# Pooled attention and token mixer on one Trainium2 core: v summed by GpSimd in fp32, with another order of the first batch and one tail unit for each of the first batches

## The chip, the cores and the metric

One core of one Trainium2 chip. The metric is the device time of one execution in microseconds (us), lower is better. Engines as in the profile: PE is TensorE (PEld its weight loads), DVE VectorE, ACT ScalarE, POOL GpSimd, SP SyncE; SPq and POOLq are DMA issues.

## What is computed

Eight batches of eight heads, 576 tokens, 64 wide. k and v are averaged over groups of eight tokens (72 pooled rows), every q row attends to the 72, and the result, laid out as x (batch, token, 512), goes through a token mix and a channel mix:

```
k_p = k.reshape(B, H, 72, 8, D).mean(axis=3);  v_p likewise
attn = softmax(q @ k_p^T / sqrt(D));  x = attn @ v_p
u = x + (relu(x^T @ w_tok1) @ w_tok2)^T
out = u + relu(u @ w_ch1) @ w_ch2
```

Inputs and output are fp32; the kernel loads everything with a cast to bf16.

## The kernel before

The 576 tokens of a batch are 512 main tokens, four (NJ) on each of 128 partitions, and a tail of 64. Two tails share 128 partitions as a group: batches 0 and 7, 1 and 2, 3 and 4, 5 and 6 (`groups`; `slot_of` gives the upper or lower half). In the group of 0 and 7 each batch has a tail unit of its own; otherwise one `TailUnit` does both batches of a group with the first.

For a batch, `pool_k` averages k with small matmuls against a 0/1/8 matrix (line 241, tails 245) and copies the result into a block form `kbd` (ACT line 250, DVE 251, from one PSUM tile). `pool_v` averages v with four matmuls of 512 columns (line 258) and one for the tail (259); ACT copies to `vpx` (260), whose last column of ones yields the softmax denominators. A `Unit` has two of the four main token sets: `do_qT`, `do_S` (scores, line 286; maximum 289 and difference 291 on DVE), `do_E` (exponential, 299), `do_PT` (transposed probabilities) and `do_AV` (`values`, line 325, then reciprocal 329 and multiply 330 on DVE). Batches 0 and 1 transpose on PE (lines 275 and 310, copies 277 and 311), later ones by DMA issued on SP (`qT_dma`, line 472; line 306).

`token_mix` has `do_AT` (lines 414 and 418, ReLU 408 and 410), `do_u` (442, tail 450, sum 447) and `do_uT` (on PE with copies at 464 for batch 0, by SP DMA at 458 otherwise). `channel_mix` has `do_GT` (line 673, ReLU 675), which needs all of `uT`, and the output matmuls (688, sum 692, stores at 707).

The instruction order on each engine is that of the program: `weave` mixes a main stream (channel mix of batch b, `c_stream`) with a side stream (values and mixes of b+1, `value_stream`; scores of b+2, `score_stream`) by weights; `delay` holds the side back at the start, `lead` ends it early. `first_stream` is the attention and token mix of batch 0 alone, and `second_stream` that of batch 1, beside the channel mix of batch 0. `keep_running` issues matmuls on zeros.

GpSimd issues all loads (line 120 main, 124 tail), in order. k, q and v have two buffers each. Batches 1 and 2 are loaded up front; a later one behind a copy (`gate`, line 658) that waits for work two batches earlier:

```python
add(0, load_gated, 3, lambda: x_main[1][:, 0, 0:1])           # in second_stream
add(0, load_gated, b + 2, lambda: c.pT[1][:, 0, 0:1])         # in value_stream
```

Of the kernel before, what the change touches and what calls it, by code (L numbers as in the profile page):

```python
# [48 lines left out]
def kernel(  # L49
# [34 lines left out]
    kv_pool = ctx.enter_context(tc.tile_pool(name="kv", bufs=2))  # L84
    tail_pool = ctx.enter_context(tc.tile_pool(name="tl", bufs=2))
# [24 lines left out]
    for t in tail_t[0]:  # L110
        nc.vector.memset(t[half[1]], 0.0)

    def load(b):
        g = group_of[b]
        if g and slot_of[b] == 0:
            tail_t[g] = [tail_pool.tile([P, H, D], BF16, name=n) for n in ("kt", "qt", "vt")]
        main_t[b] = [kv_pool.tile([P, H, NJ, D], BF16, name=n) for n in ("km", "qm", "vm")]
        for i in (0, 2, 1) if slot_of[b] else (0, 1, 2):
            src, mt, tt = (k, q, v)[i], main_t[b][i], tail_t[g][i]
            nc.gpsimd.dma_start(out=mt.rearrange("p h j d -> p h (j d)"),  # L120
                                in_=src[b, :, 0:MAIN, :].rearrange("h (p j) d -> p h (j d)", j=NJ))

            for bb in [b] if g == 0 else groups[g] if slot_of[b] == 0 else []:
                nc.gpsimd.dma_start(out=tt[half[slot_of[bb]]], in_=src[bb, :, MAIN:S, :].rearrange("h p d -> p h d"))

    main_t[0] = [kv_pool.tile([P, H, NJ, D], BF16, name=n) for n in ("km", "qm", "vm")]
# [44 lines left out]

    NB = 3
    kbd = [singles.tile([P, H, 2, SP], BF16, name=f"kbd{i}") for i in range(NB)]
    vpx = [singles.tile([SP, H, D + 1], BF16, name=f"vpx{i}") for i in range(NB)]
    for i in range(NB):
        eng = nc.vector if i == 0 else nc.any
        eng.memset(kbd[i], 0.0)
        eng.memset(vpx[i][:, :, D], 1.0)
# [4 lines left out]
    x_tail[0] = singles.tile([P, DM], BF16, name="xt0")  # L183
    nc.any.memset(x_tail[0][half[1]], 0.0)
# [47 lines left out]
    def pool_k(b):  # L232
        g, s = group_of[b], slot_of[b]
        km, kt = main_t[b][0], tail_t[g][0]
        kp_ps = ps.tile([P, HP, SP], FP32, name="pa")
        if b == 0:
            keep_running(kp_ps.rearrange("p r n -> p (r n)"), 18)
        for pr in range(HP):
            for j in range(NJ):
                for hl in range(2):  # L240
                    nc.tensor.matmul(out=kp_ps[hl * D:(hl + 1) * D, pr, 0:SPM], lhsT=km[:, 2 * pr + hl, j, :],  # L241
                                     rhs=pool_m[:, 0:SPM], start=(j == 0), stop=(j == NJ - 1))
        for pr in range(HP):
            for hl in range(2):
                nc.tensor.matmul(out=kp_ps[hl * D:(hl + 1) * D, pr, SPM:SP], lhsT=kt[:, 2 * pr + hl, :],
                                 rhs=pool_t[s][:, SPM:SP], start=True, stop=True)
        heads = kbd[b % NB].rearrange("p (r t) e n -> p r t e n", t=2)
        for hl in range(2):
            src = kp_ps[hl * D:(hl + 1) * D]
            nc.scalar.copy(out=heads[0:D, :, hl, 0, :], in_=src)  # L250
            nc.vector.tensor_copy(out=heads[D:P, :, hl, 1, :], in_=src)  # L251

    def pool_v(b):
        g, s = group_of[b], slot_of[b]
        vm, vt = main_t[b][2], tail_t[g][2]
        vp_ps = ps.tile([SP, H, D], FP32, name="pa")
        for j in range(NJ):
            nc.tensor.matmul(out=vp_ps, lhsT=pool_m, rhs=vm[:, :, j, :], start=(j == 0), stop=False)  # L258
        nc.tensor.matmul(out=vp_ps, lhsT=pool_t[s], rhs=vt, start=False, stop=True)
        nc.scalar.copy(out=vpx[b % NB][:, :, 0:D], in_=vp_ps)  # L260

    class Unit:
# [40 lines left out]
        def do_PT(self, e):  # L303
            self.pT[e] = pt_pool.tile([P, H, P], BF16, name="pT")
            if not self.by_pe:
                nc.sync.dma_start_transpose(out=self.pT[e], in_=self.probs[:, e].rearrange("p h n -> p (h n)"))
                return
            pT_ps = ps_tr.tile([SP, H, P], BF16, name="pt")
            for h in range(H):
                nc.tensor.transpose(out=pT_ps[:, h, :], in_=self.probs[:, e, h, 0:SP], identity=ident)  # L310
            (nc.scalar.copy if self.first else nc.vector.tensor_copy)(out=self.pT[e][0:SP], in_=pT_ps)  # L311

        def do_AV(self, e):
            values(self.pT[e], x_main[self.b][:, 2 * self.jj + e, :], slice(0, P), [(slice(0, P), self.b)],
                   2 if self.first else 0)

    def values(pT, xo, rows, pieces, extra, place=lambda h: h):
        w = rows.stop - rows.start
        for hf in range(2):
            ao = ps.tile([P, HP, D + 1], FP32, name="pa")  # L320
            keep_running(ao.rearrange("p h d -> p (h d)"), extra)
            for hh in range(HP):
                h = hf * HP + hh
                for r, b in pieces:
                    nc.tensor.matmul(out=ao[r, hh, :], lhsT=pT[0:SP, place(h), r], rhs=vpx[b % NB][:, h, :],  # L325
# [8 lines left out]
    class TailUnit:  # L334
# [19 lines left out]
        def do_S(self):  # L354
            w = self.rows
            sc = [ps.tile([P, HP, SP], FP32, name="pa") for _ in range(2)]
            for pr in range(HP):
                for hl in range(2):
                    for b in self.bs:
                        r = half[slot_of[b]]  # L360
                        nc.tensor.matmul(out=sc[hl][r, pr, :], lhsT=self.qT[hl * D:(hl + 1) * D, pr, r],
# [3 lines left out]
            for hl in range(2):  # L365
                mx = sm_pool.tile([P, 8], FP32, name="mx")
                nc.vector.tensor_reduce(out=mx[w, 0:HP], in_=sc[hl][w], axis=AX.X, op=ALU.max)
                sh = sh_pool.tile([P, 6, SP], FP32, name="sh")
                nc.vector.tensor_tensor(out=sh[w, 0:HP], in0=sc[hl][w],
                                        in1=mx[w, 0:HP, None].broadcast_to([w.stop - w.start, HP, SP]),  # L370
# [3 lines left out]
        def do_E(self):  # L374
            w = self.rows
            self.probs = prob_t[self.g % 2]
            for hl in range(2):
                nc.scalar.activation(out=self.probs[w, hl, :, 0:SP], in_=self.sh[hl][w, 0:HP], func=AF.Exp, scale=scale)

        def do_PT(self):  # L380
            w = self.rows
            self.pT = pt_pool.tile([P, H, P], BF16, name="pT")
            if not self.by_pe:
                nc.sync.dma_start_transpose(out=self.pT, in_=self.probs.rearrange("p e h n -> p (e h n)"))
                return
            pT_ps = ps_tr.tile([SP, H, P], BF16, name="pt")
            for h in range(H):
                nc.tensor.transpose(out=pT_ps[:, self.place(h), w], in_=self.probs[w, h % 2, h // 2, 0:SP],
                                    identity=ident[w, w])
            copy = nc.scalar.copy if self.first else nc.vector.tensor_copy  # L390
            copy(out=self.pT[0:SP, :, w], in_=pT_ps[:, :, w])

        @staticmethod
        def place(h):
            return (h % 2) * HP + h // 2

        def do_AV(self):
            values(self.pT, x_tail[self.g], self.rows, [(half[slot_of[b]], b) for b in self.bs],
                   2 if self.first else 0, self.place)

    def token_mix(b):
# [24 lines left out]
        def do_both_AT():  # L426
            at_ps = [ps.tile([P, DM], FP32, name="pa") for _ in range(2)]
            for m in range(2):
                mains(m, at_ps[m])
            for m in range(2):  # L430
                tails(m, at_ps[m])
            for m in range(2):
                acts(m, at_ps[m])
# [45 lines left out]
    def units(b):  # L479
# [4 lines left out]
        if g == 0:  # L484
# [6 lines left out]
        return parts[b]  # L491

# [3 lines left out]
    def mix_stream(st, b, pooled=()):  # L496
# [9 lines left out]
        if b == 0:  # L506
            add(2160, do_both_AT)
        else:
            add(1080, do_AT, 0)
            add(1080, do_AT, 1)  # L510
            for bb in pooled:
                add(KP, pool_k, bb)
# [7 lines left out]
    def first_stream():  # L520
# [4 lines left out]
        a, c, t = units(b)  # L525
        add(KP, pool_k, b)
        add(QT, a.do_qT, 0, HP)
# [4 lines left out]
        add(QT, c.do_qT, HP, H, copy=nc.vector.tensor_copy)  # L532
# [3 lines left out]
        add(0, c.do_E, 0)  # L536
        add(VP, pool_v, b)
        add(0, a.do_E, 1)
        add(SC, c.do_S, 1)
        add(0, a.do_E, 2)  # L540
        add(PT, a.do_PT, 0)
        add(SC, c.do_S, 2)
        add(PT, a.do_PT, 1)
        add(0, c.do_E, 1)
        add(QT, t.do_qT)
        add(AV, a.do_AV, 0)
        add(0, c.do_E, 2)
        add(SC, t.do_S)
        add(AV, a.do_AV, 1)
        add(PT, c.do_PT, 0)  # L550
        add(PT, c.do_PT, 1)
        add(AV, c.do_AV, 0)
        add(0, t.do_E)
        add(PT, t.do_PT)
        add(AV, c.do_AV, 1)
        add(AV, t.do_AV)
        mix_stream(st, b)
        return st

    def second_stream(st):  # L560
# [4 lines left out]
        add(KP, pool_k, b)  # L565
# [15 lines left out]
        add(0, load_gated, 3, lambda: x_main[1][:, 0, 0:1])  # L581
        add(SC, c.do_S, 2)
        add(0, c.do_E, 1)
        add(AV, a.do_AV, 1)
        add(0, c.do_E, 2)
        add(KP, pool_k, 2)
        add(QT, t.do_qT)
        add(PT, c.do_PT, 0)
        add(2 * SC, t.do_S)
# [5 lines left out]
        add(VP, pool_v, 2)  # L595
        add(AV, t.do_AV)
        units(2)
        add(0, qT_dma, 2)
        mix_stream(st, b)

    def owned(b):

        g, s = group_of[b], slot_of[b]
        return [b] if g == 0 else groups[g] if s == 0 and g > 1 else []

    def score_stream(st, b):
# [24 lines left out]
        for bb in own:  # L631
            add(VP, pool_v, bb)
# [23 lines left out]
    def load_gated(b, ready):  # L656

        nc.gpsimd.tensor_copy(out=gate, in_=ready())  # L658
        load(b)

    def channel_mix(uTs, us, dst, width):
# [37 lines left out]
        return [(864, do_GT(m0)) for m0 in range(0, NM, per)], out_pieces  # L699

    def c_stream(b):
# [11 lines left out]
        wide, chunk = channel_mix(uT_main[b], lambda j: u_main[b][:, j, :], dst_main, MAIN)  # L713
# [15 lines left out]
    load(2)  # L729
    engines = {mybir.EngineType.PE, mybir.EngineType.Activation, mybir.EngineType.DVE,  # L730
               mybir.EngineType.SP, mybir.EngineType.Pool}
    with tc.manual_schedule(engines=engines):
        weave(Stream(), first_stream())
        for b in range(B):
# [8 lines left out]
            weave(c_stream(b), side, 0.0 if b == 0 else 3456.0 if b == 1 else 1728.0, 3456.0 if b == B - 2 else 1728.0)  # L743
# [30 lines left out]
```

## Time and profile before

| | |
|---|---|
| Median of 3 runs | 296.34 us (295.75 to 296.78) |
| The profiled execution's own time | 295.11 us |
| Its span in the profile | 293.4 us |
| Attention and token mix of batch 0 alone | to 33.7 us |
| Channel mix of batch 0 beside the attention of batch 1 | 33.7 to 72.7 us |
| First matmul of the channel mix of batch 1 | 72.67 us |

Times in the profile are from the span's start. A timeline row has start, duration, engine, line, operation, output and inputs, and in brackets the idle time before it and what ended it. A group row has the busy time of all its instructions, the mean in ns, and the idle time before them. A stage row has the stretch, its length, then busy time and count of PE, PEld, DVE, ACT and POOL, the granted share of the PE clock, DMA share and GB/s.

### The profile page before, as it was taken

The numbers are of one execution on the slowest core, as the hardware profiler recorded it, in microseconds if no ns is written. First come the engines' busy times: TensorE is split into PE (matmuls) and PEld (weight loads), VectorE is DVE, ScalarE is ACT, GpSimd is POOL, SyncE is SP. The second block draws the span as 40 slices with busy tenths as digits, with TensorE's granted clock in tenths as the row PEclk, the third lists the DMA queues.
The fourth block names the chain that finished last, engine by engine and source line by source line (L and its number), as shares of the span: only waits on it lengthen the run. The fifth ranks groups of instructions, "written<-read, shape, count | busy, mean of one in ns | idle before, by whom it ended". The sixth has DMA issues, their size and how long they took to land.

```text
span 293.4 us, 5564 instructions
## 1 busy us (share of the span) xinstructions
PE 278.4 (95%) x2234; PEld 148.8 (51%) x2234; DVE 166.3 (57%) x382; ACT 122.5 (42%) x225; POOL 49.3 (17%) x80
## 2 busy tenths in 40 slices
PE   6778999998999999999999999999999999999994
PEld 3554555544545545456545444465445444464463
DVE  4776478868638944385558653684559642530012
ACT  7473667203652445125543445035433552026320
POOL 8656606300120008000300032000000000000000
PEclk9799999999999999999999999999999999999999
DMA  7999999996999999959998999759425920341013
GB/s 86 187 204 196 188 205 198 187 207 115 218 168 150 174 230 155 192 121 161 171 186 141 181 185 175 117 160 169 103 53 123 167 73 36 92 108 36 36 38 108
DMA packets 106843, 42.54 MB, mean 145 GB/s; under 512 B 73921, under 2 KB 102209, under 8 KB 106817
## 3 DMA queue, kind: packets, MB, share of 16 engines
q0 software_dynamic: 41392, 17.93, 49.2%
q1 hardware_dynamic: 65280, 24.13, 41.3%
q8 instruction: 17, 0.28, 0.4%
q10 hardware_dynamic: 144, 0.13, 0.1%
q14 instruction: 10, 0.07, 0.1%
HBM read 35.85 MB, written 9.44 MB: 154 GB/s over the span
## 4 chain that ended last, share of the span: by engine, by line
PE 81%; DMA 6%; ACT 5%; DVE 5%; POOL 2%; issue 1%; DVEq 0%; POOLq 0%
PE pa L673 30%; PE pa L688 28%; PE pa L414 4%; PE pa L442 4%; PE pa L325 3%; DMA vm<-in_v_dram 3%; PE pa L258 2%; DMA qT<-qm 2%; PE pa L286 2%; ACT pT L311 1%; DMA uTm<-um 1%; PE pa L450 1%; DVE mx L289 1%; PE pa L241 1%; DVE sh L291 1%; PE pa L418 1%
## 5 line engine op out<-in xcount | busy, mean ns | idle before, releaser
L688 PE MATMUL pa<-wc,GT 128*128 128x512 bf16 (+1 forms) x444 | 104.4, 373 | 0.0
L673 PE MATMUL pa<-uTm,wc 128*128 128x512 bf16 x384 | 92.9, 379 | 1.3 <-DMA uTm<-um 1.3
L675 ACT ACTIVATE GT<-pa 128x512 bf16<-128x512 f32 x108 | 64.5, 597 | 69.6 <-PE pa L673 69.5
L673 PEld LDWEIGHTS <-wc 128*128 128x128 bf16 x576 | 45.8, 98 | 38.4 <-DVE mx L289 1.7
L688 PEld LDWEIGHTS <-GT 128*128 128x128 bf16 x444 | 41.6, 98 | 40.5
L299 ACT ACTIVATE prob_m<-sh 128x432 bf16<-128x432 f32 (+1 forms) x48 | 24.4, 521 | 53.6 <-DVE sh L291 34.0
L692 DVE TENSOR_TENSOR o<-pa,um 128x512 f32<-128x512 f32 (+1 forms) x33 | 22.2, 672 | 31.0 <-PE pa L688 30.9
L289 DVE TENSOR_REDUCE mx<-pa 128x6 f32<-128x432 f32 (+1 forms) x48 | 26.4, 550 | 4.6 <-PE pa L286 4.5
L291 DVE TENSOR_TENSOR sh<-pa,mx 128x432 f32<-128x432 f32 (+1 forms) x48 | 26.8, 558 | 3.7
L330 DVE TENSOR_TENSOR xm<-pa,den 128x256 bf16<-128x256 f32 x64 | 27.2, 425 | 2.3
L329 DVE RECIPROCAL den<-pa 128x4 f32<-128x4 f32 (+1 forms) x74 | 13.0, 176 | 22.8 <-PE pa L325 22.8
L447 DVE TENSOR_TENSOR um<-pa,xm 128x512 bf16<-128x512 f32 x30 | 20.1, 687 | 5.5 <-PE pa L442 5.4
L325 PEld LDWEIGHTS <-pT 72*128 72x128 bf16 (+1 forms) x320 | 14.4, 100 | 9.3 <-issue 2.1
L442 PE MATMUL pa<-AT,w2m 128*128 128x512 bf16 x64 | 18.1, 379 | 0.5 <-ACT AT L408 0.5
L410 DVE TENSOR_SCALAR AT<-pa 128x512 bf16<-128x512 f32 x8 | 5.5, 692 | 22.2 <-PE pa L418 22.2
L658 POOL COPY gate<-pT 128x1 bf16<-128x1 bf16 x4 | 0.8, 188 | 102.6 <-DMA pT<-prob_m 102.6
L286 PE MATMUL pa<-kbd,qT 128*128 128x144 bf16 x128 | 16.3, 234 | 1.0 <-DMA qT<-qm 0.5
L325 PE MATMUL pa<-vpx,pT 72*128 72x65 bf16 (+1 forms) x320 | 16.6, 194 | 0.4 <-ACT pT L311 0.4
L286 PEld LDWEIGHTS <-qT 128*128 128x128 bf16 x128 | 11.2, 101 | 10.8 <-ACT qT L277 1.2
L414 PE MATMUL pa<-xm,w1m 128*128 128x512 bf16 x64 | 16.3, 379 | 0.0
L251 DVE CAST kbd<-pa 64x288 bf16<-64x288 f32 x16 | 7.3, 456 | 12.1 <-ACT kbd L250 12.0
L230 PE MATMUL pa<-idle 128*128 128x288 bf16 (+2 forms) x44 | 10.8, 366 | 2.2 <-DVE pool_t L159 2.2
(99 smaller groups left out, 211.5 us busy)
## 6 DMA issues: line engine op xcount, KB each, us to landing
out_dram<-o SPq DMA_DIRECT2D x31, 256.0 KB, 2.5
km<-in_k_dram POOLq DMA_DIRECT2D x8, 512.0 KB, 7.8
vm<-in_v_dram POOLq DMA_DIRECT2D x8, 512.0 KB, 10.6
qm<-in_q_dram POOLq DMA_DIRECT2D x7, 512.0 KB, 10.0
wc<-in_moe_w_ch_dram POOLq DMA_DIRECT2D x6, 512.0 KB, 10.7
out_dram<-o SPq DMA_DIRECT2D x9, 128.0 KB, 2.4
kt<-in_k_dram POOLq DMA_DIRECT2D x8, 64.0 KB, 6.5
qm<-in_q_dram POOLq DMA_DIRECT2D x2, 256.0 KB, 5.1
```

What stands on the lines that cost most here:

```text
L286: nc.tensor.matmul(out=sc[:, (h - h0) * 2:(h - h0) * 2 + 2, :], lhsT=qTs[self.b][:, 2 * h + self.jj, :], rhs=kbd[self.b % NB][:, h], start ...
L289: nc.vector.tensor_reduce(out=mx[:, 0:n], in_=sc, axis=AX.X, op=ALU.max)
L291: nc.vector.tensor_tensor(out=sh[:, 0:n], in0=sc, in1=mx[:, 0:n, None].broadcast_to([P, n, SP]), op=ALU.subtract)
L299: nc.scalar.activation(out=self.probs[:, :, h0:h1, 0:SP].rearrange("p e h n -> p h e n"), in_=self.sh[i][:, 0:(h1 - h0) * 2].rearrange("p ...
L325: nc.tensor.matmul(out=ao[r, hh, :], lhsT=pT[0:SP, place(h), r], rhs=vpx[b % NB][:, h, :], start=True, stop=True)
L330: nc.vector.tensor_tensor(out=xo[rows, hf * HP * D:(hf + 1) * HP * D].rearrange("p (h d) -> p h d", d=D), in0=ao[rows, :, 0:D], in1=den[ro ...
L414: nc.tensor.matmul(out=at_ps, lhsT=w1m[:, j, m * P:(m + 1) * P], rhs=x_main[b][:, j, :], start=(j == 0), stop=False)
L442: nc.tensor.matmul(out=u_ps, lhsT=w2m[:, m, j, :], rhs=ATs[b][:, m, :], start=(m == 0 and not by_act), stop=(m == 1))
L673: nc.tensor.matmul(out=g_ps[:, i, :], lhsT=wc1[:, kk, m * P:(m + 1) * P], rhs=uTs[:, kk, :], start=(kk == 0), stop=(kk == 3))
L675: nc.scalar.activation(out=GT[:, m0:m0 + per, :], in_=g_ps, func=AF.Relu)
L688: nc.tensor.matmul(out=hold["ps"], lhsT=GT[:, kk, j * P:(j + 1) * P], rhs=wc2[:, kk, cols], start=(kk == 0), stop=(kk == NM - 1))
L692: nc.vector.tensor_tensor(out=o_sb, in0=hold["ps"], in1=us(j)[:, cols], op=ALU.add)
```

## The change

- v of batches 2 to 7 is loaded with eight consecutive tokens on each of 72 partitions, main and tail in one transfer of 1.18 MB read, into a pool `vs` with one buffer that all batches share (batches 0 and 1 use half of it). `sum_v` adds the eight tokens on GpSimd: for each pair of heads three adds of 512, 256 and 128 elements a partition, the last writing `vpx` in bf16. `pool_v` stays for batches 0 and 1. `vpx` now holds sums, not means, and its last column 8 instead of 1.
- The load of batch 3 is split: k and q up front, behind the loads of batch 2; v after the sums of batch 2, with its own sums behind it, without the gate. `load_gated` ends with the sums of its batch.
- Batches 1 and 2 have a tail unit each. A single tail lays its even heads on partitions 0 to 63 and its odd heads on 64 to 127, so that one maximum, one difference, one exponential and four transposes do it instead of two, two, two and eight.
- `pool_k` writes the two head parities to two PSUM tiles; ACT copies one, DVE the other.
- In the first batch another order: more `keep_running` matmuls ahead of and behind pooled k (28 and 6 in place of 18), the tail earlier, values with one PSUM tile for all eight heads and another for the denominators, the token mix begun on the first finished pairs, the four `do_u` in a row, pooled k of batch 1 among the `uT` transposes, and the first three channel-mix tiles in two halves of tokens.
- Pooled k of batch 2 moves from the middle of `second_stream` to its token mix. The side stream beside the channel mix of batch 0 starts with a `delay` of 3456 instead of 0.

```diff
+    v_pool = ctx.enter_context(tc.tile_pool(name="vp", bufs=1))
+    sum_pool = ctx.enter_context(tc.tile_pool(name="sums", bufs=1))
...
+            if i == 2 and b > 1:
+                vs = v_pool.tile([P, H, POOL, D], BF16, name="vs")
+                nc.gpsimd.dma_start(out=vs[0:SP].rearrange("p h t d -> p h (t d)"),
+                                    in_=src[b].rearrange("h (p t) d -> p h (t d)", t=POOL))
...
-            keep_running(kp_ps.rearrange("p r n -> p (r n)"), 18)
+            keep_running(kp_ps[0].rearrange("p r n -> p (r n)"), 28)
...
+    def sum_v(b):
+        vs, add = main_t[b][2][0:SP], ALU.add
+        for h0 in range(0, H, 2):
+            hs = slice(h0, h0 + 2)
+            s4 = sum_pool.tile([P, 2, 4, D], FP32, name="s4")[0:SP]
+            nc.gpsimd.tensor_tensor(out=s4, in0=vs[:, hs, 0:4], in1=vs[:, hs, 4:8], op=add)
+            nc.gpsimd.tensor_tensor(out=s4[:, :, 0:2], in0=s4[:, :, 0:2], in1=s4[:, :, 2:4], op=add)
+            nc.gpsimd.tensor_tensor(out=vpx[b % NB][:, hs, 0:D], in0=s4[:, :, 0], in1=s4[:, :, 1], op=add)
...
-            (nc.scalar.copy if self.first else nc.vector.tensor_copy)(out=self.pT[e][0:SP], in_=pT_ps)
+            by_dve = e == 0 and self.jj == 1 if self.first else e == 1
+            (nc.vector.tensor_copy if by_dve else nc.scalar.copy)(out=self.pT[e][0:SP], in_=pT_ps)
...
+                        dst = sc[hl][r, pr, :] if len(sc) > 1 else sc[0][half[hl], pr, :]
...
-        if g == 0:
+        if g < 2:
             t = TailUnit(g, [b])
...
 (first_stream, after the values of the first unit)
+        add(AV, t.do_AV)
+        add(1080, do_both_AT, (0, 1), False, False)
+        add(AV, c.do_AV, 0)
+        add(AV, c.do_AV, 1)
+        add(1080, do_both_AT, (2,), True, False)
+        add(540, do_both_AT, (3,), False, True)
+        for j in range(NJ):
+            add(690, do_u, j)
+        add(224, do_uT, 0)
+        add(224, do_uT, 1)
+        k1 = []
+        add(KP, lambda: k1.append(pool_k_sum(1)))
+        add(224, do_uT, 2)
+        add(224, do_uT, 3)
+        add(0, lambda: pool_k_copy(1, k1[0]))
...
 (second_stream)
-        add(0, load_gated, 3, lambda: x_main[1][:, 0, 0:1])
+        add(0, load, 3, (2,))
+        add(0, sum_v, 3)
...
-        add(KP, pool_k, 2)
-        add(VP, pool_v, 2)
-        mix_stream(st, b)
+        mix_stream(st, b, owned(2))
...
-        for bb in own:
-            add(VP, pool_v, bb)
...
-        load(b)
+        load(b, (0, 2, 1) if slot_of[b] else (0, 1, 2))
+        sum_v(b)
...
+        wide = [(432, do_early(m, hold, *t)) for t in ((0, width // 2), (width // 2, width)) for m in range(early)]
...
     load(2)
+    load(3, (0, 1))
+    sum_v(2)
...
-            weave(c_stream(b), side, 0.0 if b == 0 else 3456.0 if b == 1 else 1728.0, 3456.0 if b == B - 2 else 1728.0)
+            weave(c_stream(b), side, 3456.0 if b <= 1 else 1728.0, 3456.0 if b == B - 2 else 1728.0)
```

## The prediction

> **What bounds the kernel now.** I read the engine shares and the 40 slices first, then busy time by stage, then the groups of what goes away, then the timelines of the first batch and of GpSimd (POOL).
>
> ```profile
> PE 278.4 (95%) x2234; PEld 148.8 (51%) x2234; DVE 166.3 (57%) x382; ACT 122.5 (42%) x225; POOL 49.3 (17%) x80
> PE   6778999998999999999999999999999999999994
> DMA  7999999996999999959998999759425920341013
> ```
>
> TensorE (PE) is full from the sixth slice on. The DMA engines are full too, up to about 62 us: while both are full, loads land in a fixed order at a fixed pace.
>
> ```profile
> 33.70:72.67 38.97, 36.06 (x325) 19.56 (x321) 28.92 (x64) 17.64 (x34) 9.14 (x13) 1.00 1.32 181
> 72.67:104.73 32.06, 31.90 (x272) 16.09 (x273) 21.18 (x49) 15.22 (x29) 2.83 (x4) 1.00 1.17 186
> 104.73:136.60 31.87, 31.87 (x237) 17.10 (x236) 18.56 (x42) 12.35 (x22) 6.94 (x10) 1.00 1.09 163
> ```
>
> Busy time by stage (PE, PEld, DVE, ACT, POOL). From 72.7 us on PE idles 0.2 us in a stage of 32, so PE work removed there is time gained. The stage before (channel mix of batch 0 beside attention of batch 1) has 2.9 us of idle PE, and the first 33.7 us, before any channel mix, are paced by latencies.
>
> ```profile
> L258 PE MATMUL pa<-vm,pool_m 128*72 128x512 bf16 x32 | 8.2, 379 | 0.4 <-DMA vm<-in_v_dram 0.4
> L259 PE MATMUL pa<-vt,pool_t 128*72 128x512 bf16 x8 | 3.0, 379 | 0.0
> L212 POOL COPY w2m<-w2r 128x512 bf16<-128x512 bf16 x2 | 1.2, 635 | 3.0 <-DMA w2r<-in_moe_w_tok_dram 3.0
> L214 POOL COPY w2t<-w2r 128x128 bf16<-128x128 bf16 x2 | 0.5, 283 | 0.0
> ```
>
> The v pooling costs five matmuls of 512 columns a batch. The two POOL copies are the nearest rows for the new sums.
>
> **The sum, part by part.**
>
> *v pooling off PE.* In the chain of waits four such matmuls take 0.86 us (start to start 0.216 each, not the 379 ns of one, which overlap), so a batch costs 5 x 0.216 = 1.08. Six batches leave PE. Those of 3 to 7 start after 72.7 us: 5 x 1.08 = **-5.4**. That of batch 2 runs at 55.5, in the stage of batch 0: **-1.1**. The ACT copies of 0.58 that go with them are beside other work.
>
> *Single tails.* The tail of batches 1 and 2 was one unit. Now each has its own, its even and odd heads on the two partition halves. Score and value matmuls are as many, the second batch's share moving one stage on (AV 8 x 0.02 to 0.03). The 8 PE transposes of batch 1's tail become 4: 4 x 0.056, **-0.25**. DVE does two more reciprocals and two more multiplies (2 x 0.17 + 2 x 0.42 = 1.2 us), in a stage where it is 66% busy (21.18 of 32.06): nothing. SP gets two more transposes (tail q and tail probabilities of batch 2, 1.2 to 1.4 us each), counted below.
>
> *First batch.* The v of batch 0 lands at 13.8 and gates the values; q and k were earlier.
>
> ```profile
> 13.78 1.02 PE L258 MATMUL pa<-vm,pool_m 128*72 128x512 bf16 x4 [0.36 <-DMA vm<-in_v_dram]
> 28.14 0.60 ACT L408 ACTIVATE AT<-pa 128x512 bf16<-128x512 f32 x1 [3.32 <-PE pa L418]
> 33.71 1.02 PE L673 MATMUL pa<-uTm,wc 128*128 128x512 bf16 x4
> ```
>
> Start of v pooling, of the first ReLU of the token mix, of channel mix. I walked the new order with the durations of the rows. ACT: vpx 0.58 to 15.5, exponentials and tail q to 16.9, two pT copies (0.96) to 19.4, exponentials to 20.9, tail pT (0.58), last pT to 23.1, while DVE takes one of the four. The token mix starts on finished pairs and ends near 26.3, its ReLU near 26.9: 1.3 earlier. The four u then run without transposes between them (10 matmuls, 2.15 us, to 29.0); two transposes, pooled k of batch 1 (0.7), two more, and channel mix starts on the first half of uT at 30.8. The old order also had pooled k of batch 1 ahead of 33.7. That is 2.9 by hand. Against it stand ten more warm-up matmuls (18 took 4.5 us, so up to 2.4 more, ending near 8.8, where k landed at 7.2) and six of 512 columns; they end near q's landing or up to 1 us past it, in front of v's 13.8. Granted clock was 0.50 from 11 to 13 us, and the warm-up may keep it at 1.0. Four more memsets (0.3 to 0.4 each) lie beside the first loads. Bounds +1 and -4; I take **-2.5**.
>
> *Waits at the end of batch 0's stage.*
>
> ```profile
> 65.90 0.36 PEld L286 LDWEIGHTS <-qT 128*128 128x128 bf16 x6 [1.00 <-DMA qT<-qm]
> 72.67 3.61 PE L673 MATMUL pa<-uTm,wc 128*128 128x512 bf16 x16 [1.27 <-DMA uTm<-um]
> ```
>
> PE waits for SP transposes, of which the first took 4.78 us there (1.8 in later stages) beside loads in flight to 64 us. Now k and q of batch 3 are issued earlier, and its v is the only load after about 59: the transposes meet less traffic, but one more (tail q) stands ahead of them on SP, and batch 1's attention starts 3.5 us of channel mix later, so DVE's 28.9 us (26.6 now: two pT copies of 0.69 go to ACT, two of pooled k, 0.46, to the first batch) fill a shorter stage. Bounds -2.5 and +2; I take **-0.9**.
>
> *The sums on POOL.* Each batch has 12 adds: four times 512, 256 and 128 elements. The two copies give 0.92 ns an element and 0.17 fixed. At one read an element a batch costs 4 x (0.64 + 0.40 + 0.28) = 5.3 us; at two reads 4 x (1.11 + 0.64 + 0.40) = 8.6. No row has a two-input add, so both stay; I take 8.6, as each add reads two operands.
> The Trainium skill (GPSIMD Engine Reference, "Elementwise — side-by-side cycle accounting") has about 2.6 cycles at 1.2 GHz for a two-input element: by it 3584 x 2.17 ns and the same fixed cost would be 9.8 us, an estimate.
>
> What waits behind them: one v buffer makes POOL wait for v2, add, issue v3, wait, add, and only then pass the gate to the loads of batch 4.
>
> ```profile
> 52.67 0.69 POOL L124 DMA_DIRECT2D vt<-in_v_dram  x1 [0.31 <-DMA qm<-in_q_dram]
> 55.31 0.68 POOL L124 DMA_DIRECT2D vt<-in_v_dram  x1 [1.96 <-DMA km<-in_k_dram]
> 79.58 0.19 POOL L658 COPY gate<-pT 128x1 bf16<-128x1 bf16 x1 [23.59 <-DMA pT<-prob_m]
> 80.09 0.89 POOL L120 DMA_DIRECT2D km<-in_k_dram  x1 [0.33 <-PE pa L325]
> ```
>
> q2 landed at 52.7 and k3 at 55.3: 2.6 us for each full load. v2 now follows q2, with three tails fewer ahead: it lands near 52. Adds to 60.6, v3 issued and landed (7.6 us, as k4 did from 80.1 to 87.7) by 68.2, adds to 76.8, k4 issued at 77.3, landed at 84.9. PE reaches the pooling of k4, at 92.7 before, some 5 us earlier: 87 to 88. So **0**, with 2 to 3 us to spare; each us over about 10 in a batch's adds costs two. In later stages adds have 32 us a batch, and POOL was idle 24 to 29 us before each gate. v's load has 576 rows of 2 KB instead of 1024 of 1 KB and 512 of 256 bytes: no dearer, unless 72 partitions use fewer engines; its landing of 8 to 16 us is inside that slack later on.
>
> Sum: 5.4 + 1.1 + 0.25 + 2.5 + 0.9 = 10.15. The profiled execution took 295.1 us (span 293.4), so 285.0 by its own time; the median of the runs is 1.2 higher: **286.2**.
>
> **Rivals.**
> 1. *Only the matmuls count* (0.2). First batch and transpose waits return what they gain: DVE's 26.6 us in a stage of some 36, less the 3.5 of its later start, speak for it; against it, the longest idle PE there came from transposes, not from DVE. 5.4 + 1.1 + 0.25 gives 289.6.
> 2. *The adds become a late load, slower than before* (0.1). If a batch's adds take T, k4 lands at 67.7 + 2T, and PE stands still in front of its pooling from T = 10 on, with all behind it. T = 15 eats the 10 us; T = 17 gives 300. For it: no row of an add, and dependent adds wait for each other. Against it: that is twice what the copies give for two reads.
> The same stall would come if DVE held off GpSimd: the Trainium skill (SBUF — State Buffer, "Who interferes with whom") has the two share a port pair, locked for instructions in a 2-port mode or with two SBUF inputs. In the groups nearly all DVE work reads PSUM.
> 3. *A milder late load*, T of 11 to 13 (0.1): 2 to 6 us returned, 288 to 292.
>
> That the sums leave PE is certain from the code. Forecast 0.6. The range 283.5 to 291.5 reaches from the better bounds of the first batch and the waits (about 2.7 more) over rivals 1 and most of 3; outside it are rival 2 and a tail above or below. About 0.3% (0.9 us) is what a measurement here can tell from no change. Faster: forecast, rival 1 and most of 3, 0.87; within 0.3%: a T near 15, 0.03; slower: rival 2, 0.10.
>
> **What would show it.** L258 and L259 8 and 2 times instead of 32 and 8; 24 new adds of each size on POOL, a batch in 5 to 10 us; the first channel-mix matmul near 31 and that of batch 1 near 67; the pooling of k4 without a wait for DMA. Wrong if PE waits for k4 or for a sum before a values matmul, or if idle PE in the stage of batch 0 grows past 4 us.

## The result and the profile after

The changed kernel is slower: 303.77 us (median of 4, 303.47 to 306.38) against 296.04 of the kernel before, ratio 1.0285, 95% interval 1.0218 to 1.0353. The forecast was 286.2 us, its range 283.5 to 291.5. The profiled execution took 306.38 us (span 304.7). Some of the variants below fall into two groups of executions some 4.5 us apart, and one execution of the last variant took 314.68 us at a granted clock of 0.883: ratios leave out executions over 1.5% above the fastest of their kernel, medians are those of all.

The page after: engine shares, then the 40 slices of 7.6 us.

```profile
PE 277.5 (91%) x2249; PEld 150.0 (49%) x2249; DVE 163.2 (54%) x372; ACT 120.4 (40%) x221; POOL 100.8 (33%) x145
PE   7978009897999999999999999999999999999995
PEclk9999855997999999999999999999999999999999
DMA  8999999940779997999899979997904870152013
```

Two slices of PE are empty behind the fourth, and the granted clock falls to a half behind them, and to 0.7 once more in the tenth. From the eleventh slice on PE is full as before, so most of the loss is in one place; PE's timeline shows it:

```profile
30.35 0.69 PE L262 MATMUL pa<-pool_m,km 128*64 128x64 bf16 x32
46.26 0.38 PE L266 MATMUL pa<-pool_t,kt 128*64 128x8 bf16 x8 [15.22 <-DMA kt<-in_k_dram]
46.57 1.03 PE L526 MATMUL pt<-ident,um 128*128 128x128 bf16 x8
47.40 5.21 PE L781 MATMUL pa<-uTm,wc 128*128 128x256 bf16 x24
```

Pooled k of batch 1 starts at 30.35, as the walk in the prediction had it. Its main part runs; its tail (line 266) stands for 15.22 us, and two of the transposes and the channel mix of batch 0 stand behind it. POOL's timeline has the load that it waits for:

```profile
29.93 0.89 POOL L133 DMA_DIRECT2D km<-in_k_dram  x1
32.50 0.69 POOL L137 DMA_DIRECT2D kt<-in_k_dram  x1 [1.67 <-DMA qm<-in_q_dram]
55.53 0.89 POOL L133 DMA_DIRECT2D qm<-in_q_dram  x1 [8.78 <-PE pa L321]
66.05 1.15 POOL L293 TENSOR_TENSOR s<-vs 72x512 f32<-72x512 bf16 x1 [7.74 <-DMA vs<-in_v_dram]
67.27 0.72 POOL L294 TENSOR_TENSOR s<-s 72x256 f32<-72x256 f32 x1
68.08 0.46 POOL L295 TENSOR_TENSOR vpx<-s 72x128 bf16<-72x128 f32 x1
```

The load at 32.50 is the k tail of batch 2. It fills the upper half of `kt1`; the tail matmul of batch 1 reads all 128 partitions of that tile, with zeros in `pool_t` for the half that isn't its own. The kernel before had issued both halves with batch 1:

```profile
20.98 1.38 POOL L124 DMA_DIRECT2D kt<-in_k_dram  x2
```

It is one line of the change that gives the second half to the load of batch 2:

```diff
- for bb in [b] if g == 0 else groups[g] if slot_of[b] == 0 else []:
+ for bb in [b] if g < 2 else groups[g] if slot_of[b] == 0 else []:
```

The late start also holds back q of batch 3 (8.78) and v of batch 2, whose buffer is free only when PE has pooled v of batch 1. So the sums begin at 66 instead of the 52 of the forecast; without the late start they begin at 57 to 58 (below), so 5 to 6 us of this have another reason.

Stages after (columns as before: PE, PEld, DVE, ACT, POOL, clock, DMA share, GB/s):

```profile
47.40:89.20 41.80, 38.84 (x318) 22.17 (x317) 25.70 (x59) 19.14 (x35) 17.59 (x22) 0.90 0.72 104
89.20:119.70 30.50, 30.36 (x272) 15.41 (x271) 22.71 (x52) 13.26 (x26) 15.74 (x22) 1.00 1.12 186
119.70:152.10 32.40, 32.40 (x240) 17.28 (x239) 20.03 (x46) 13.03 (x24) 14.43 (x19) 1.00 1.11 180
47.40:52.40 5.00, 5.00 (x26) 3.57 (x25) 1.16 (x3) 2.35 (x5) 0.00 (x0) 0.50 1.95 183
```

The stage of batch 0 takes 41.8 us. In its first 5 us the granted clock is 0.50, and it falls once more behind a wait of 1.68 us, to 0.50 from 74 to 76:

```profile
72.39 0.44 PE L382 MATMUL pa<-vpx,pT 72*64 72x65 bf16 x8 [1.68 <-DVE pT L446]
```

From batch 1's channel mix to PE's last end it took 212.0 us (89.2 to 301.2), before 216.8 (72.7 to 289.5): 4.8 less, of 5.4 forecast.

### The profile page after: what moved, and what is told of

Its sections match the earlier page's. It is cut to its first block, busy times and chain, and to the rows that moved or that the text cites. A ratio compares the mean times of both kernels' runs of the same rounds, so it can differ in the third digit from the quotient of the medians.

```text
span 304.7 us, 5672 instructions
## 1 busy us (share of the span) xinstructions
PE 277.5 (91%) x2249; PEld 150.0 (49%) x2249; DVE 163.2 (54%) x372; ACT 120.4 (40%) x221; POOL 100.8 (33%) x145
## 4 chain that ended last, share of the span: by engine, by line
PE 79%; DMA 11%; DVE 4%; POOL 4%; issue 1%; ACT 0%; DVEq 0%; POOLq 0%
PE pa L765 30%; PE pa L750 29%; DMA kt<-in_k_dram 5%; PE pa L468 4%; PE pa L506 4%; DMA qm<-in_q_dram 3%; DMA w2r<-in_moe_w_tok_dram 3%; PE pa L382 3%; PE pa L321 2%; PE pa L781 2%; PE pa L514 1%; DVE sh L326 1%; PE pa L262 1%; PE pa L472 1%; DVE xm L387 1%; DVE mx L324 1%
## 5 line engine op out<-in xcount | busy, mean ns | idle before, releaser
L750 PE MATMUL pa<-uTm,wc 128*128 128x512 bf16 x372 | 89.8, 379 | 0.0
L752 ACT ACTIVATE GT<-pa 128x512 bf16<-128x512 f32 x105 | 62.0, 597 | 61.9 <-PE pa L750 61.7
L765 PEld LDWEIGHTS <-GT 128*128 128x128 bf16 x444 | 41.6, 98 | 40.9 <-issue 0.8
L293 POOL TENSOR_TENSOR s<-vs 72x512 f32<-72x512 bf16 x24 | 27.6, 1150 | 52.4 <-DMA vs<-in_v_dram 51.0
L387 DVE TENSOR_TENSOR xm<-pa,den 128x256 bf16<-128x256 f32 x56 | 23.8, 425 | 1.9
L386 DVE RECIPROCAL den<-pa 128x4 f32<-128x4 f32 (+1 forms) x66 | 11.7, 177 | 18.4 <-PE pa L382 18.2
L294 POOL TENSOR_TENSOR s<-s 72x256 f32<-72x256 f32 x24 | 17.4, 723 | 1.9
L382 PEld LDWEIGHTS <-pT 72*128 72x128 bf16 (+1 forms) x280 | 12.6, 100 | 9.7 <-DVE pT L446 1.8
L266 PE MATMUL pa<-pool_t,kt 128*64 128x8 bf16 x64 | 2.3, 176 | 15.2 <-DMA kt<-in_k_dram 15.2
L382 PE MATMUL pa<-vpx,pT 72*128 72x65 bf16 (+1 forms) x280 | 14.1, 194 | 1.7 <-DVE pT L446 1.7
L468 PE MATMUL pa<-xm,w1m 128*128 128x512 bf16 x56 | 15.3, 397 | 0.0
```

The costliest lines, as they stand in the source:

```text
L293: nc.gpsimd.tensor_tensor(out=s4, in0=vs[:, hs, 0:4], in1=vs[:, hs, 4:8], op=add)
L382: nc.tensor.matmul(out=ao[r, hh, :], lhsT=probs_of(h, r), rhs=vpx[b % NB][:, h, :], start=True, stop=True)
L387: nc.vector.tensor_tensor(out=xo[rows, hf * HP * D:(hf + 1) * HP * D].rearrange("p (h d) -> p h d", d=D), in0=ao[rows, :, 0:D], in1=den[ro ...
L468: nc.tensor.matmul(out=at_ps, lhsT=w1m[:, j, m * P:(m + 1) * P], rhs=x_main[b][:, j, :], start=(j == 0), stop=False)
L750: nc.tensor.matmul(out=g_ps[:, i, :], lhsT=wc1[:, kk, m * P:(m + 1) * P], rhs=uTs[:, kk, :], start=(kk == 0), stop=(kk == 3))
L752: nc.scalar.activation(out=GT[:, m0:m0 + per, :], in_=g_ps, func=AF.Relu)
```

## The experiments

Every kernel but the second holds the edit of the first, so that the wait of 15 us is out of the way. The kernel before took a median of 295.0 to 295.4 us beside them.

### The 15 us

**Own half.** The tail matmul of a group whose second batch comes later reads its own half alone:

```diff
+ w = half[s] if g == 1 else slice(0, P)
- nc.tensor.matmul(..., lhsT=kt[:, 2 * pr + hl, :], rhs=pool_t[s][:, SPM:SP], ...)
+ nc.tensor.matmul(..., lhsT=kt[w, 2 * pr + hl, :], rhs=pool_t[s][w, SPM:SP], ...)
```

> The tail of k of batch 1 is pooled from its own 64 partitions alone, so that it no longer reads the half of the shared tile that the load of batch 2 fills. Theory A (the pooling of k of batch 1 waits 15.2 us for the tail of batch 2, since both lie in one tile and the matmul reads all 128 partitions): the wait goes, and with it the half clock behind it (24 half-width channel-mix matmuls took 5.2 us in place of 2.6): 303.8 - 15.2 - 2.6 = about 286 us, channel mix of batch 0 from about 32 us. Rival B (the wait is for batch 1's own load, or it only moves to the next use of a late load): 300 us or more.

Median 295.51 of four: 290.97 once, 295.48 to 296.51 three times. PE's timeline, of an execution of 295.55:

```profile
31.27 0.29 PE L267 MATMUL pa<-pool_t,kt 64*64 64x8 bf16 x8
31.95 2.78 PE L782 MATMUL pa<-uTm,wc 128*128 128x256 bf16 x24
```

The wait is gone, and the 24 matmuls that took 5.21 us now take 2.78: the other 2.4 were the half clock behind the wait.

**Both tails early.** The matmul as in the change; instead both k tails are loaded with batch 1, as before the change:

```diff
- for bb in [b] if g < 2 else groups[g] if slot_of[b] == 0 else []:
+ both = g > 1 or (g == 1 and i == 0)
+ for bb in (groups[g] if slot_of[b] == 0 else []) if both else [b]:
```

> The matmul stays as it is, on all 128 partitions, but both k tails of the shared tile are loaded with batch 1, as before the change. Theory A: the same wait goes by another way; one more tail transfer (0.4 us) stands ahead of q and v of batch 1: 286 to 287 us. Rival B: 300 us or more.

Median 293.95 (291.66, 291.73, 296.18, 296.29); ratio 0.9864 (0.9809 to 0.992). Channel mix starts at 31.6. The two edits reach the wait from its two ends, reader and load, and either alone removes it: the cause is shown. Even the shorter executions of both stay 4 us and more over the forecast, which leaves a second question.

### The parts

**v back on PE.** The first batch, the single tails and the new order alone: `vs` and `sum_v` go, v has two buffers again and `pool_v` serves all batches. The load of batch 3 stays split.

```diff
- add(0, sum_v, 3)
...
+ for bb in own:
+     add(VP, pool_v, bb)
```

> As e1_own_half, but v of all batches is pooled on TensorE as before the change (its tail for batches 1 and 2 on their own halves): new first batch and single tails alone. The prediction's terms: six batches of 1.08 us are back, so 6.5 us over e1_own_half, about 292.5. Rival (the sums' late loads eat what they bring): equal to e1_own_half or under it.

296.32 (10 runs, 294.57 to 298.0), ratio 1.0029 (0.9994 to 1.0063): nothing gained. Channel mix starts at 31.5, 2.2 us before that of the kernel before, yet batch 1's starts at 72.3 against 72.7. The head's gain is lost within one stage, which takes 40.8 us in place of 39.0; 1.0 of it is more PE work (37.07 against 36.06), the rest idle. From there to PE's last end it takes 217.4 us (72.3 to 289.8), no less than the 216.8 before. So the other parts bring nothing that reaches the end, and what the change does bring comes with the sums.

**Every sum twice.**

```diff
- for h0 in range(0, H, 2):
+ for h0 in list(range(0, H, 2)) * 2:
```

> As e1_own_half, with every sum on GpSimd done twice, so that a batch takes 20.6 us in place of 10.3; the result is the same. By the prediction's rival 2, k of batch 4 then lands near 67.7 + 2 x 20.6 = 109 us where TensorE wants it near 88: some 20 us over e1_own_half, about 306. If the sums have slack that the prediction did not see: under 292.

322.17, ratio 1.0911 (1.0853 to 1.097). PE's timeline:

```profile
77.92 0.23 PE L383 MATMUL pa<-vpx,pT 72*128 72x65 bf16 x2 [3.10 <-POOL vpx L296]
112.84 1.07 PE L262 MATMUL pa<-pool_m,km 128*64 128x64 bf16 x32 [15.56 <-DMA km<-in_k_dram]
```

The late load of rival 2 is real: with twice the adds the pooling of k4 waits 15.56. That it took 16 us more than expected goes with the values matmuls, which wait for sums six times, 12.5 us in total. With the adds of the change (10.1 us a batch) there is no such wait: with both tails early, k4 was issued at 85.90 and landed 6.2 later, at 92.1, and its pooling ran at 95.60 without a wait for a DMA. (The pooling ahead of it, at 87.48, is that of k of batch 3.) That leaves 3.5 us of slack, and 8.0 in the first kernel (landed at 92.0, pooled at 99.94); 2 to 3 were forecast.

### The other 4 us

In the first kernel's execution of 295.55, SP, POOL and PE ahead of batch 1's channel mix:

```profile
40.95 0.85 POOL L126 DMA_DIRECT2D vs<-in_v_dram  x1 [2.19 <-PE pa L322]
57.63 1.15 POOL L294 TENSOR_TENSOR s<-vs 72x512 f32<-72x512 bf16 x1 [8.06 <-DMA vs<-in_v_dram]
64.11 4.76 SPq L523 DMA_TRANSPOSE uTm<-um  x3
67.20 0.86 POOL L126 DMA_DIRECT2D vs<-in_v_dram  x1
68.98 6.17 SPq L342 DMA_TRANSPOSE pT<-prob_m  x2
75.75 1.15 POOL L294 TENSOR_TENSOR s<-vs 72x512 f32<-72x512 bf16 x1 [7.20 <-DMA vs<-in_v_dram]
75.88 1.01 PE L751 MATMUL pa<-uTm,wc 128*128 128x512 bf16 x2 [5.93 <-DMA uTm<-um]
77.22 2.63 SPq L342 DMA_TRANSPOSE pT<-prob_m  x2
```

The load of v2 goes out at 40.95, its sums start at 57.63. The last transposes of u are issued by 68.9, the load of v3 at 67.2 (landed at 75.6); PE waits 5.93 for the former. Its clock is 0.60 from 75.9 to 82.7. The execution of 291.73 with both tails early has the same in small, with the load of v3 at 66.87 and a clock of 0.57 from 72.5 to 76.5:

```profile
72.52 4.00 PE L751 MATMUL pa<-uTm,wc 128*128 128x512 bf16 x10 [2.73 <-DMA uTm<-um]
31.60:72.50 40.90, 35.02 (x318) 20.32 (x316) 28.72 (x65) 20.41 (x38) 17.07 (x22) 1.00 1.41 178
```

Two ideas: transposes and load hold each other up in the DMA engines, or the transposes are only too late on SP.

**v3 later.** The load of v3 waits for the last transposed u of batch 1; k4 and q4 are issued ahead of its sums.

```diff
+ def late_v():
+     nc.gpsimd.tensor_copy(out=gate, in_=uT_main[1][:, 0, MAIN - 1:MAIN])
+     load(3, (2,))
+     load(4, (0, 1))
+     sum_v(3)
```

> As e1_own_half, but v of batch 3 is loaded only when the uT transposes of batch 1 have landed, and k and q of batch 4 are issued ahead of the sums of batch 3. Theory C (in e1_own_half the first channel-mix matmul of batch 1 waits 5.9 us, in e2_both_tails 2.7, because the transposes share the DMA engines with that load, and half clock follows): last transpose lands 2.5 us after its issue, channel mix of batch 1 from about 71.5 us without half clock; 212 us remain from there as in the changed kernel, so 287 to 289 us. Rival D (the transposes are late because SP issues them late, 1.6 us each, whatever else is in flight): the start stays at 72.5 to 76 and the time at 291 to 295.

299.18, ratio 1.0135 (1.0106 to 1.0164), worse. But batch 1's channel mix starts at 71.1 without a wait: the transposes of u land 2.8 us after their issue (median of four), where they took 4.3 beside the load of v3 in the first kernel. The loads, now at 71 to 73.5, meet the next transposes:

```profile
69.53 2.62 SPq L342 DMA_TRANSPOSE pT<-prob_m  x2
74.76 7.72 SPq L342 DMA_TRANSPOSE pT<-prob_m  x2
```

Two transposes of probabilities held SP for 2.62 us as the loads were only being issued and 7.72 beside them, and values wait 1.91, 2.90 and 2.40 us for them. In the first kernel such a pair took 6.17 beside the load of v3 and 2.63 behind its landing. The pairs of 2.62 and 6.17 both stand right behind three transposes of u, so their place on SP isn't the reason. The kernel with every sum twice says the same: its load of v3 is issued at 76.51, and batch 1's channel mix starts at 70.85 without a wait. The wait moves with the load, so the transposes are held up by the load beside them; rival D, by which only SP's order counts, doesn't hold.

**PE kept busy in the wait.** 14 matmuls of 512 columns on zeros ahead of batch 1's channel mix.

```diff
+ if b == 1:
+     st.add(0, lambda: warm(14))
```

> As e1_own_half, with 14 matmuls of 512 columns on zeros (3.0 us) ahead of the channel mix of batch 1, where TensorE waits for the transposes anyway. If the half clock behind that wait is a cost of its own: the clock stays at 1.0 there and the time is 1.5 to 3 us under that of e1_own_half in the executions where the wait is long (295.5), near 292. If the half clock costs nothing: no difference, or up to 3 us more where the wait is short.

292.59 (291.52 to 294.03), ratio 0.9914 (0.9885 to 0.9942). PE's timeline, of the execution of 291.52:

```profile
69.75 3.18 PE L248 MATMUL pa<-idle 128*128 128x512 bf16 x14
72.77 2.54 PE L751 MATMUL pa<-uTm,wc 128*128 128x512 bf16 x11
```

The clock is at 1.00 throughout the stage of batch 1. So the wait is paid twice without these matmuls, in idle time and then in half clock; the time that PE spends in it stays. The times of this kernel lie between the shorter and the longer ones of the first two.

**v2 in another buffer.** v of batch 2 goes into the second `GT512` buffer, free until about 72 us, so batch 3 is loaded whole up front.

```diff
+ vs = (gt_pool.tile([P, NM, MAIN], BF16, name=f"GT{MAIN}")[:, 0:H].rearrange(...) if b == 2 else v_pool.tile(...))
...
- load(3, (0, 1))
+ load(3)
```

> As e1_own_half, but v of batch 2 lies in the second channel-mix buffer, which is free until 72 us, so that v of batch 3 needs no finished sums and is loaded whole with its k and q, up front. Theory C (the single v buffer puts the load of v3 among the transposes that channel mix and values of the next batches need): that load is over by about 65 us, the first channel-mix matmul of batch 1 comes at 70 to 72 us with a short wait and no half clock, and k of batch 4 is early: 286 to 289 us. Rival D (traffic of transposes among themselves and on SP): no better than e1_own_half's shorter executions, 291.

291.45 (290.42 to 291.59), ratio 0.9862 (0.9844 to 0.988). The load of v3, issued at 50.0, lands only 22.6 us later, so the transposes of u still run beside it (6.76 us on SP for three):

```profile
74.58 3.61 PE L751 MATMUL pa<-uTm,wc 128*128 128x512 bf16 x16 [2.12 <-DMA uTm<-um]
```

The wait for u is 2.12, with 0.90 and 1.81 for q ahead of it, and batch 1's channel mix starts at 74.6, later than with both tails early, not at the 70 to 72 expected. What makes up for it is the clock, 1.00 behind the wait: 211.9 us from there to PE's last end. Transposes of q and tail q, issued at 49.1 to 56.7, now share the DMA engines with the longer train of loads, which move 0.13 MB from 54 to 56 us; in the kernel before, without transposes beside them, they moved 0.38.

**q transposes later**, behind the first output store, with the buffer of the last experiment and without it:

```diff
+ if b == 1:
+     add(0, qT_dma, 2)
...
- add(0, qT_dma, 2)
```

> As e10_v2_in_gt, with the transposes of q of batch 2 issued behind the first store of the output (about 58 us) in place of about 49. Theory E (transposes in flight beside loads slow both: loads moved about 390 KB in 2 us before 52 us and 90 to 190 KB from there until 70, while in the kernel before, with the q transposes at 58.8, they kept 360 to 395 KB until 60): loads end near 61, uT transposes land by 68 to 69, channel mix of batch 1 starts at about 70 us without a wait, 212 us remain: 287 to 288.5 us. Rival F (the wait is of SP's own order, each transpose 1.2 to 1.6 us after the last): the later q transposes push those of uT back and the time is over that of e10_v2_in_gt, 292 or more.

> As e1_own_half, with the same later q transposes alone; v of batch 3 still follows the sums of batch 2. Theory E: k and q of batch 3 land by 59 us, v of batch 3 is issued near 62 and meets the uT transposes, so part of the wait stays: 289 to 291 us, without the long executions of 295.5. Rival F: 292 or more.

290.35, ratio 0.9837 (0.9812 to 0.9863), with the buffer; 295.01 (292.27 to 296.59), ratio 0.9976 (0.9944 to 1.0009), without. In the first, q comes late (PE waits 3.44 for it, and the clock behind it is 0.57 from 66 to 70); in the second, u (5.27, in the execution of 296.59). Moving transposes along SP alone moves the wait.

**No delay.** Three of these kernels with the side stream's `delay` at 0 again, as before the change.

> As e7_v3_late, with the side stream beside the channel mix of batch 0 from the start (delay 0, as before the change). If the start of batch 1's channel mix hangs on when its u and their transposes come (theory C and D alike), they come earlier by up to 3 us and the wait there goes: 1 to 2 us under e7_v3_late. If DVE or TensorE set it: no difference.

> As e10_v2_in_gt, with delay 0 beside the channel mix of batch 0. In e9_late_no_delay this brought the start of batch 1's channel mix from 71.1 to 69.5 us, without a wait. If that start still carries to the end: 1 to 2 us under e10_v2_in_gt, 285 to 287. If the transposes, now earlier, run into the last loads: equal or over it.

> As e12_v2_in_gt_q_later with delay 0: u and its transposes come 2 to 3 us earlier, near the end of the loads. Theory E: within 1 us of e12_v2_in_gt_q_later, since the loads, not u, then set the transposes. If the start of u sets it: 1 to 2 us under.

299.09, ratio 1.0138 (v3 later); 296.39, ratio 0.9919 (v2 in another buffer); 292.92, ratio 0.9919 (with q later): none better than its partner at 3456 (1.0135, 0.9862, 0.9837). In an execution of 296.32 of the second, PE still waits 5.61 from 71.3. So in these three kernels the delay isn't the cause.

**u of batch 1 on PE.** 16 transposes on PE with copies in place of four on SP, with the v2 buffer and without it:

```diff
- if b > 0:
+ if b > 1:
```

> As e10_v2_in_gt, with u of batch 1 transposed on TensorE as in batch 0 (16 transposes of 0.056 us, four copies of about 0.5 us shared by ACT and DVE) in place of four DMA transposes. Theory G (in every version the end of this stage, 71 to 77 us, is set by the DMA engines, which must finish loads and transposes; whichever transpose comes last is waited for): with four of them gone TensorE enters the channel mix of batch 1 near 71 to 72 us without a wait, after the remaining waits for q of batch 2: 287 to 289 us. Rival H (TensorE and DVE set the stage, the waits only take the place of other idle time): 290.5 to 292, as e10_v2_in_gt with 0.9 us more work.

> As e1_own_half, with the same uT on TensorE. Theory G: the wait of 2.7 to 5.9 us for uT, the half clock behind it and the long executions of 295.5 go: 287 to 290 us, all close together; v of batch 3, now against the probability transposes alone, may return a little. Rival H: 291 and over, still two groups.

290.03 (289.18 to 290.91), ratio 0.9814 (0.9778 to 0.9849), with the buffer: the lowest median of all, though its interval overlaps those of the others with the buffer, and faster than both kernels. 291.31, ratio 0.9841 (0.9809 to 0.9874), without: five of its six executions took 290.44 to 291.37, the sixth 314.68, and only that one was profiled. PE at the end of the stage, then the stages of the kernel with the buffer, from its execution of 289.18:

```profile
69.59 1.89 PE L766 MATMUL pa<-wc,GT 128*128 128x512 bf16 x8
71.32 1.89 PE L751 MATMUL pa<-uTm,wc 128*128 128x512 bf16 x8
```

```profile
31.40:71.30 39.90, 35.49 (x328) 21.37 (x332) 27.29 (x62) 20.08 (x37) 17.72 (x23) 1.00 1.36 177
71.30:101.70 30.40, 29.91 (x267) 15.39 (x271) 22.41 (x53) 13.36 (x26) 20.69 (x27) 1.00 1.17 181
```

No wait at the start of channel mix, and the clock stays at 1.00. PE is still idle 4.4 us in the stage (39.9 less 35.49), spread over smaller waits. Those that the timeline names add up to 4.2 us, and none is for a DMA: 1.68 for the copy of the tail's probabilities on DVE, 1.27 for exponentials on ACT, 0.91 for the sums of u on DVE and 0.32 of issue.

## Why the prediction was wrong

**The step that failed** is pooled k of batch 1, costed as work that only changes place ("pooled k of batch 1 (0.7)", and "The old order also had pooled k of batch 1 ahead of 33.7"). It stood for 15.22 us, and the half clock behind it cost another 2.4. The landing of k of batch 1 was in time; that its tail matmul reads the whole tile, and that the diff takes the other half's load away from batch 1, was not looked at. The place of the step isn't what did it: that half landed near 46.2 us, so at its old place (32.96) the step would have stood for some 13 us too, an estimate from these times. No rival had this wait either; the sign went with it.

By its own execution the forecast was 285.0, and 306.4 came: 21.4 too little. By stage:

| | forecast | after | both tails (291.7) | own half (295.6) | v2 buffer, u on PE (289.2) |
|---|---|---|---|---|---|
| channel mix of batch 0 starts | 31.2 | 47.4 | 31.6 | 31.9 | 31.4 |
| stage of batch 0 | 36.7 | 41.8 | 40.9 | 44.0 | 39.9 |
| from batch 1's channel mix to PE's last end | 211.4 | 212.0 | 214.1 | 214.5 | 211.9 |

The forecast column is the prediction's terms on the times before: 33.7 - 2.5; 39.0 - 1.1 - 0.25 - 0.9; 216.8 - 5.4. (By these terms batch 1's channel mix starts at 67.9, not "near 67".)

- *v pooling off PE, -5.4*: about right: -4.8 measured, and -4.9 in the best kernel; with v back on PE that stretch gains nothing (217.4).
- *First batch, -2.5*: right in its place, 31.4 to 31.9 against 33.7 once the wait is out.
- *Waits at the end of batch 0's stage, -0.9 (bounds -2.5 and +2)*: mis-sized, and outside its bounds. Before, PE is idle 2.9 us in that stage. With the wait of 15 us mended it is 5.9 in the execution of 291.7 (40.9 less 35.02), so +3.0, and 8.9 in that of 295.6 (44.0 less 35.12), so +6.0. Half clock behind it costs 1.7 (4.0 us at 0.57) and 2.7 more (6.8 us at 0.60), estimates from the clock. With u transposed on PE it is 4.4, +1.5. The argument "its v is the only load after about 59: the transposes meet less traffic" is what failed: that load was on its way just when the transposes of u were.
- *Why it was*: "v2 now follows q2 [...] it lands near 52" overlooked that the one v buffer holds v of batch 1 until PE has pooled it (39.11 in own half; with both tails early the trace names this matmul, line 285, as what ended the wait ahead of the load). The load of v2 went out at 40.95, behind k of batch 3, and the adds began at 57.6. With adds of 10.1 us in place of 8.6 the load of v3 left at 67.2, where 60.6 was forecast.
- *PE work saved in that stage, -1.1 and -0.25*: about right. 36.06 fell to 35.12; in the best kernel 35.49 holds 16 more transposes (0.9 by the 0.056 each of the prediction). What failed there is idle time, not work.
- *Sums, 8.6 us a batch*: 10.1 measured (batch 3 in the first kernel, 75.75 to 85.89). The argument on k4 held: landing (92.1) and pooling (95.6, both tails) came 7 and 8 us later than forecast, and k4 wasn't waited for.
- *Rival 1 (only the matmuls count, 289.6)* is what happens once the 15 us are mended: 290.03 to 291.45 in the better kernels, and v on PE shows the head's gain returned in full. Its reason, DVE, was the smaller part: the long waits were for DMA transposes, and DVE is behind 2.6 of the 4.4 us that stay where those are gone.

What stays open is how much of the remaining 4.4 us another order of the side stream would save, and why the wait for u is 2.73 us in one execution and 5.93 in another. No kernel here reached the 286.2 of the forecast.

## What to carry to other kernels

When a diff splits a load, or moves a step, list every tile that the step's instructions read, whole tiles with the halves that are multiplied by zero, and find the load of each part. When a buffer is shared, ask who must leave it before a load can start. A gain at the head of a stage was lost here where DMA transposes set the stage's end. When a wait moves each time its load or transpose is moved, take one of the two users off the resource.

## What the runs showed of the hardware

- **Zeros don't spare a wait.** A matmul over 128 partitions waited 15.22 us for a load that fills 64 of them, where its other operand is zero.
- **Two-input adds on GpSimd**, 72 partitions: 1150, 723 and 456 ns for 512, 256 and 128 elements, so 1.81 ns an element ((1150 - 456) / 384) and 0.22 us fixed; with the gaps a batch takes 10.1 us. In the changed kernel no add took over 1155, 729 and 470 ns, so nothing shows that DVE held one off. The estimate of 9.8 in the prediction, from the Trainium skill (GPSIMD Engine Reference, "Elementwise — side-by-side cycle accounting"), was nearer than the 8.6 from the copies; its slope of 2.17 ns is higher than the one measured.
- **DMA transposes and loads slow each other.** Two transposes of probabilities held SP for 2.63 us behind the landing of v3's load, 6.17 beside the load of v3 and 7.72 beside three loads. The loads moved 0.13 MB in 2 us beside transposes of q and 0.38 without them.
- **Half clock after a wait late in the kernel.** Behind 15.22 us of idle PE the clock stayed at 0.50 to 52.4; behind 5.93 us the next 6.8 us had 0.60. Matmuls on zeros in the wait kept it at 1.00. The Trainium skill (TensorE: Matmul & The Clock Gate, "HAM oscillation — how this bites in real kernels") has idle gaps over about 3.4 us bring this on, with which these two waits agree. Shorter waits did it too: 2.73 us were followed by 4 us at 0.57 (both tails) and 1.68 us by half clock from 74 to 76 (changed kernel), while 2.12 us left the clock at 1.00 (v2 in another buffer). So in these runs 3.4 us is no bound for a single wait.
